# Reading a flag into the engines' registers at the point where it is made, instead of at the end of the kernel

## The chip, the cores and the metric

The kernel runs on one core of one Trainium2 chip. The metric is device time in microseconds (us). It is taken as the median of several executions; before the change three executions took 930.01, 934.81 and 933.51 us, so the median is 933.51 us. One further execution was profiled; its span, from the first instruction to the last, is 929.1 us.

## What is computed

Two blocks follow each other, for 4 sequences (batch 4) of 768 tokens.

The first block is attention with routing, for 8 heads of width 64. Each query and key is assigned to the nearest of 16 centroids, and a query sees only keys of its own cluster. The second block is a feed-forward layer on the joined heads (width 512, hidden width 2048), with a layer norm in front and a residual sum behind:

```python
q_assign = np.argmax(np.einsum('bhsd,hcd->bhsc', q_n, c_n), axis=-1)
k_assign = np.argmax(np.einsum('bhsd,hcd->bhsc', k_n, c_n), axis=-1)
mask = q_assign[:, :, :, None] == k_assign[:, :, None, :]
scores = np.where(mask, scale * q @ k^T, -1e9)
attn = softmax(scores) @ v                     # (B,H,S,D) -> x: (B,S,512)
xn = (x - mu) / np.sqrt(var + 1e-06) * g_ln
out = x + np.maximum(xn @ w_ch1, 0.0) @ w_ch2
```

## The kernel before, in words

**The fast path and its flag.** The kernel computes everything in a fast form that holds only for ordinary inputs: no ties between clusters, and softmax denominators in a safe range. While it runs it collects evidence: `hits` (counts from the routing) and `rdens` (the reciprocals of the denominators). The function `all_in_range()` (lines 735 to 754) folds these into one number, the flag: eleven small VectorE (DVE) instructions make one column `ends` of 128 values, TensorE (PE) turns the column into a row in PSUM (`flag_ps`, L749), and DVE takes its minimum (`flag_f`, L751) and casts it to an integer (`flag`, L753). At the very end the kernel reads the flag (L1008) and, if it is 0, recomputes everything in a slow, general way (`general`, L1009 to 1011). With the inputs of the reference the flag is 1, and the general part does not run.

**Reading the flag.** `nc.values_load` gives every engine that must branch a register with the flag. It is not one instruction but one TENSOR_LOAD on each of the five instruction streams (PE, DVE, ACT, POOL, SP), each of which waits until the cast L753 has run. On SP two bounds instructions follow it. The branches of L1009 and L1010 stand at the end.

**The order of the work.** First comes attention, for 16 pairs of heads, until about 343 us; with it the weights are converted from 64-bit floats. Then comes the feed-forward part, one sequence b after the other (b = 0 to 3). Within a sequence there is a first layer (L774 matmuls, eight units) and a second layer (L867 matmuls). Both use a scheme of fewer block products, at the price of extra sums of blocks on DVE. In the second layer each of six parts (numbered 1, 2, 5, 6, 7, 4, 3 in the order of use, with part 1 ahead of the loop) multiplies three row tiles, 8 matmuls each, so that a part is 24 matmuls of the program. In the trace each of these 32-bit matmuls is two MATMUL records, 48 a part.

**Who sets the order.** Most of the first layer of b = 0 stands in a block of its own whose order is written out for PE, DVE and ACT. All of the rest of the feed-forward part, from the second layer of b = 0 to the end, stands under `tc.manual_schedule(engines={mybir.EngineType.PE})`. That means: PE keeps the order in which the program is written, and the order of DVE, ACT, POOL and SP is chosen by a planner from the dependences. An instruction for PE that is written at some place inside this block therefore stands at that place in PE's stream. The flag load of the kernel before stands behind the block, and so the planner places it on all five streams.

**Around the change.** Between part 1 and part 2 of the second layer of b = 0 the program writes, in this order: the sums `hidden_sums(c, False)` (L861, L862, L863 on DVE), the weight sum `w2_sum(st, 2)` (L851 on DVE), `all_in_range()`, the loads for the norm of the next sequence (`norm_load`, `rows_load`), and then the parts 2, 5, 6, 7, 4, 3. Part 2 is the `y_ps` matmuls of L867, part 5 the first `z_ps` ones, and parts 6, 7 and 4 add to `x_ps`. The next sequence's norm statistics (L537, L538 on DVE, from the tiles `xr` that SP loads with L529) are mixed into this stretch; so is the addition of the residual (L878, L890 on DVE) and the store of the output (L882 on SP).

Of the kernel before, what the change touches and what calls it, by code (L numbers as in the profile page):

```python
# [19 lines left out]
def kernel(  # L20
# [11 lines left out]
    nc = tc.nc  # L32
# [23 lines left out]
    def pool(name, bufs, **kw):  # L56
        return stage.enter_context(tc.tile_pool(name=name, bufs=bufs, **kw))
# [12 lines left out]
    def ps(name, dt=F32, n=512):  # L70
        return pools["t"].tile([P, n], dt, tag="t", name=name)
# [449 lines left out]
    def norm_load(b):  # L521
        xn = norm_tiles(b)[0]
        for c in range(NDC):
            nc.sync.dma_start(out=xn[:, c, :], in_=xT_d[b][c])
# [70 lines left out]
    def w1_sums(b, j, which=range(4)):  # L595
        if 0 in which:
            t = xpool.tile([P, 4, NDH, P], F32, tag="ws", name="ws", bufs=2)
            sets[b, j] = {"s": [t[:, i] for i in range(4)], "all": t}
        t = sets[b, j]["all"]
        for i, (x, op, y) in enumerate((  # L600
            (w1_block(1, 0, j), ALU.add, w1_block(1, 1, j)),
            (t[:, 0], ALU.subtract, w1_block(0, 0, j)),
            (w1_block(0, 0, j), ALU.subtract, w1_block(1, 0, j)),
            (w1_block(0, 1, j), ALU.subtract, t[:, 1]),
        )):
            if i in which:
                nc.vector.tensor_tensor(t[:, i], x, y, op)
# [127 lines left out]
    def all_in_range():  # L735
        ends = small.tile([P, 2], F32, tag="ends", name="ends")
        every = rdens.rearrange("p r e -> p (r e)")

        nc.vector.tensor_reduce(ends[:, 0:1], every, AX.X, ALU.add)
        nc.vector.tensor_reduce(ends[:, 1:2], every, AX.X, ALU.min)  # L740
        nc.vector.tensor_single_scalar(ends[:, 0:1], ends[:, 0:1], WIDE, op=ALU.is_le)
        nc.vector.tensor_single_scalar(ends[:, 1:2], ends[:, 1:2], 1.0 / WIDE, op=ALU.is_ge)
        nc.vector.tensor_tensor(ends[:, 0:1], ends[:, 0:1], ends[:, 1:2], ALU.min)
        for op, op1 in ((ALU.max, ALU.is_le), (ALU.min, ALU.is_ge)):
            nc.vector.tensor_reduce(ends[:, 1:2], hits, AX.X, op)
            nc.vector.tensor_single_scalar(ends[:, 1:2], ends[:, 1:2], float(NG), op=op1)
            nc.vector.tensor_tensor(ends[:, 0:1], ends[:, 0:1], ends[:, 1:2], ALU.min)
        fp = ps("flag_ps")
        nc.tensor.transpose(fp[:1, :P], ends[:, 0:1], ident)  # L749
        flag_f = small.tile([1, 1], F32, tag="flag_f", name="flag_f")  # L750
        nc.vector.tensor_reduce(flag_f, fp[:1, :P], AX.X, ALU.min)  # L751
        flag = const.tile([1, 1], I32, name="flag")
        nc.vector.tensor_copy(flag, flag_f)  # L753
        return flag
# [45 lines left out]
    def relu(m):  # L800
        for h in summed[:m]:
            nc.scalar.activation(h, h, AF.Relu)  # L802
        del summed[:m]
# [35 lines left out]
    def w2_sum(st, i):  # L839
        if i in (1, 3):  # L840
            st["t", i] = xpool.tile([P, NFH, MH], F32, tag="sums", name=f"w2t{i}", bufs=2)
        elif i == 2:
            st["t", 2] = xpool.tile([P, NFH, MH], F32, tag="sums", name="w2t2", bufs=2)
        o, x, y = {
            1: lambda: (st["t", 1], w2_block(0, 1), w2_block(0, 0)),
            2: lambda: (st["t", 2], w2_block(1, 1), st["t", 1]),
            3: lambda: (st["t", 3], w2_block(1, 1), w2_block(0, 1)),
            4: lambda: (st["t", 2], w2_block(1, 0), st["t", 2]),
        }[i]()
        for c in range(0, NFH, 2):  # L850
            nc.vector.tensor_tensor(o[:, c : c + 2], x[:, c : c + 2], y[:, c : c + 2], ALU.subtract)  # L851
# [41 lines left out]
    def second_layer(b, tt, part, st):  # L893
        if part == 1:
            st["x", tt] = ps("x_ps")
            second_product(st["x", tt], tt, (0, 0), w2_block(0, 0), True)
            st["p1", tt] = add_rows(b, 0, tt, 0, st["x", tt])
        elif part == 2:
            y = ps("y_ps")
            second_product(y, tt, (0, 1), w2_block(1, 0), True)  # L900
            add_store(b, 0, tt, 0, st["p1", tt], y)
        elif part == 5:
            st["z", tt] = ps("z_ps")
            second_product(st["z", tt], tt, (1, 0), st["t", 1], True)
        elif part == 6:
            second_product(st["x", tt], tt, (0, 0), st["t", 2], False)
            st["u2", tt] = add_rows(b, 0, tt, 1, st["x", tt])
        elif part == 7:
            second_product(st["x", tt], tt, ("s3",), st["t", 3], False)
            st["u3", tt] = add_rows(b, 1, tt, 1, st["x", tt])  # L910
            add_store(b, 1, tt, 1, st["u3", tt], st["z", tt])
        elif part == 4:
            second_product(st["x", tt], tt, (1, 1), st["t", 2], False)
            store(b, 1, tt, 0, add_rows(b, 1, tt, 0, st["x", tt]))
        elif part == 3:
            second_product(st["z", tt], tt, (0, 1), w2_block(1, 1), False)
            add_store(b, 0, tt, 1, st["u2", tt], st["z", tt])


    def first_units(b, j):  # L920

        chunks = within.pop(j, []) if b == 0 else []
        for part, ahead in ((1, 0), (2, 0), (4, 1), (6, 0), (3, 1), (5, 0), (7, 0)):
            if chunks and part in (1, 3):
                split_weight(chunks[0])
            if j >= ahead:
                first_layer(b, j - ahead, part)
            if part in (4, 6, 3):
                relu(1)
            if chunks and part in (2, 3):  # L930
                m = chunks.pop(0)
                join_weight(m)
                load_weight(m + 2)

            if part == 5 and j + 1 < NFH:
                w1_sums(b, j + 1)
# [18 lines left out]
    with tc.manual_schedule(engines={mybir.EngineType.PE}):  # L955
        for b in range(B):
            st = {}
            if b:
                w1_sums(b, 0)
                for j in range(NFH):  # L960
                    first_units(b, j)
            else:
                rest.close()
                ffn = pool("ffn", 2)
            relu(len(summed))
            w2_sum(st, 1)
            more = b + 1 < B
            for tt in range(TH):
                second_layer(b, tt, 1, st)
                if tt == 0:  # L970
                    first_layer(b, NFH - 1, 4)
                    first_layer(b, NFH - 1, 3)
            relu(len(summed))
            for c in range(NFH):
                hidden_sums(c, False)
            w2_sum(st, 2)
            if b == 0:
                flag = all_in_range()
            if more:
                norm_load(b + 1)  # L980
                rows_load(b + 1, 0)
            for part in (2, 5, 6, 7, 4, 3):
                for tt in range(TH):
                    second_layer(b, tt, part, st)
                    if part == 6 and tt == 0 and more:
                        norm_stat_rows(b + 1)
                if part == 2:
                    for c in range(NFH):
                        hidden_sums(c, True)
                if part == 5:  # L990
                    w2_sum(st, 3)
                if part == 6:
                    w2_sum(st, 4)
                if more and part in (2, 5):
                    for tt in range(TH):
                        norm_rows(b + 1, (0 if part == 2 else TH) + tt)
                    if part == 5:
                        norm_stats(b + 1)
                if more and part == 7:
                    for i in range(2):  # L1000
                        for c in range(NDC):
                            norm_apply(b + 1, i, c)
                if more and part == 4:
                    for i in range(1, 5):
                        x_sum(b + 1, i)

    stage.close()
    usual = nc.values_load(flag[0:1, 0:1], min_val=0, max_val=1)  # L1008
    with tc.If(usual == 0):  # L1009
        with tc.For_i(0, B, 1) as b:  # L1010
            general(tc, b, q, k, v, out, cT, rev, eps, ident, g_sb, w1, w2)
# [194 lines left out]
```

## Time and profile before

| what | value |
|---|---|
| median of three executions | 933.51 us (930.01 to 934.81) |
| span of the profiled execution | 929.1 us |
| DVE busy | 614.6 us (66%) |
| ACT busy | 349.8 us (38%) |
| POOL busy | 78.3 us (8%) |
| PE busy from 400 us to 900 us | all of it, in every stretch asked for |
| last matmul ends | about 924.2 us |
| last DVE instruction (`o_sb`, L890) | 924.18 to 924.61 us |

The page gives the busy time of each engine and its share of the span. Its "chain that ended last" follows the work back from the last instruction: at each step to what released it, or to the instruction before it on the same engine. The view of waits lists, for an engine, whom it stood still for, with the total, the number of times and the longest. A timeline lists instructions in order: start, length, engine, line, operation, output and input tiles, how many are merged in the row, and in square brackets any idle time before it. A "q" behind the engine's name (PEldq, DVEq) means the engine's instruction queue, which handles register loads and the issue of transfers; these are not counted as busy time of the engine. PEld is PE's loading of weights, which runs beside its matmuls.

### The profile page before, as it was taken

Reading aid. Unit: us, or ns where it says so; the run is one execution under the profiler, and the core shown is the slowest. Engines: PE = TensorE matmul, PEld = TensorE weight load, DVE = VectorE, ACT = ScalarE, POOL = GpSimd, SP = SyncE. Lnnn points to the kernel's source line nnn. Section 1 sums busy time; section 2 is a strip of 40 time slices with the busy share of each in tenths; the row PEclk is TensorE's granted clock in tenths of the full one; section 3 lists DMA queues with packets and bytes.
Section 4 is the critical chain, followed back from the end, with each engine's and each line's share of the span. In section 5 each row is a group of like instructions: output and inputs, shape, how many; then the busy total and the mean of one; then the engine's idle time right before and its main releaser. Section 6 shows DMA issues by size and latency. Waiting matters only on the chain.

```text
span 929.1 us, 12604 instructions
## 1 busy us (share of the span) xinstructions
PE 918.7 (99%) x4670; PEld 589.1 (63%) x4670; DVE 614.6 (66%) x1104; ACT 349.8 (38%) x551; POOL 78.3 (8%) x146
## 2 busy tenths in 40 slices
PE   8999999999999999999999999999999999999997
PEld 5444444444444445568886558886557887556886
DVE  4988999999899978889772436472346372434331
ACT  4677777767777653330003331002331001332000
POOL 2121222211211112110000000000000000000000
PEclk9999999999999999999999999999999999999999
DMA  7576888999888455645530002120002021000011
GB/s 153 128 162 125 183 177 166 210 185 166 175 175 162 100 119 142 159 91 170 176 112 8 1 0 94 55 74 17 1 0 86 18 96 40 0 1 6 30 46 37
DMA packets 177061, 89.35 MB, mean 96 GB/s; under 512 B 144096, under 2 KB 160592, under 8 KB 176992
## 3 DMA queue, kind: packets, MB, share of 16 engines
q1 hardware_dynamic: 167648, 73.06, 32.8%
q0 software_dynamic: 7744, 15.02, 8.1%
q8 instruction: 39, 0.64, 0.3%
q10 hardware_dynamic: 1600, 0.39, 0.2%
q14 instruction: 30, 0.25, 0.1%
HBM read 62.52 MB, written 17.52 MB: 86 GB/s over the span
## 4 chain that ended last, share of the span: by engine, by line
PE 92%; DVE 3%; DMA 3%; issue 1%; SPq 1%; ACT 0%; DVEq 0%; ACTq 0%
PE x_ps L867 18%; PE x_ps L774 18%; PE s_ps L407 13%; PE a_ps L419 12%; PE z_ps L867 9%; PE z_ps L774 9%; PE y_ps L867 4%; PE y_ps L774 4%; PE den_ps L456 1%; DMA v_sb<-in_v_dram 1%; PE sim_ps L313 1%; DVE es L436 1%; DMA raw<-in_moe_w_ch_dram 1%; PE simT_ps L329 1%; PE oh_ps L355 1%
## 5 line engine op out<-in xcount | busy, mean ns | idle before, releaser
L402 ACT ACTIVATE e<-s_ps 128x768 f32<-128x768 f32 x192 | 151.6, 811 | 24.3 <-PE s_ps L407 21.8
L407 PE MATMUL s_ps<-t,t 64*128 64x384 f32 x768 | 155.1, 483 | 0.0
L436 DVE TENSOR_TENSOR es<-es,e 128x768 f32<-128x768 f32 x128 | 122.7, 958 | 13.4
L419 PE MATMUL a_ps<-e,v_sb 128*64 128x384 f32 x768 | 130.9, 490 | 0.0
L419 PEld LDWEIGHTS a_ps<-e,v_sb 128*64 128x64 f32 x768 | 52.3, 137 | 70.0 <-issue 59.0
L794 DVE TENSOR_TENSOR h<-z_ps,u 128x384 f32<-128x384 f32 x64 | 35.6, 557 | 91.7 <-PE z_ps L774 69.2
L407 PEld LDWEIGHTS s_ps<-t,t 64*128 64x128 f32 x768 | 68.1, 188 | 35.0 <-issue 34.4
L867 PE MATMUL x_ps<-w2t,h 128*128 128x256 f32 x384 | 84.5, 379 | 0.0
L802 ACT ACTIVATE h<-h 128x384 f32<-128x384 f32 x96 | 49.5, 522 | 85.8 <-DVE h L794 85.8
L867 PEld LDWEIGHTS x_ps<-w2t,h 128*128 128x128 f32 x384 | 72.8, 190 | 10.1
L407 PE MATMUL s_ps<-m,mask 64*128 64x384 bf16 x192 | 62.1, 324 | 1.6 <-ACT e L402 1.2
L407 PE MATMUL s_ps<-mask,m 64*128 64x384 bf16 x192 | 62.0, 324 | 0.4 <-DVE mask L378 0.4
L789 ACT COPY u<-x_ps 128x384 f32<-128x384 f32 x64 | 30.6, 478 | 75.1 <-PE x_ps L774 75.1
L878 DVE TENSOR_TENSOR o_sb<-x_ps,xb 128x256 f32<-128x256 f32 x48 | 20.2, 422 | 49.8 <-PE x_ps L867 49.8
L789 ACT COPY p<-x_ps 128x384 f32<-128x384 f32 x32 | 14.9, 467 | 97.4 <-PE x_ps L774 97.4
L774 PE MATMUL x_ps<-xn,w 128*128 128x384 f32 x128 | 46.6, 487 | 0.6 <-ACT late L445 0.6
L774 PE MATMUL x_ps<-xt,ws 128*128 128x384 f32 x128 | 46.6, 487 | 0.0
L774 PE MATMUL x_ps<-xt,w 128*128 128x384 f32 x128 | 46.5, 486 | 0.0
L774 PE MATMUL x_ps<-xn,ws 128*128 128x384 f32 x128 | 46.5, 486 | 0.0
L774 PE MATMUL z_ps<-xt,ws 128*128 128x384 f32 x128 | 46.5, 486 | 0.0
L774 PE MATMUL z_ps<-xn,ws 128*128 128x384 f32 x128 | 46.5, 486 | 0.0
L774 PE MATMUL y_ps<-xn,w 128*128 128x384 f32 x128 | 46.5, 486 | 0.0
(147 smaller groups left out, 1350.7 us busy)
## 6 DMA issues: line engine op xcount, KB each, us to landing
raw<-in_moe_w_ch_dram SPq DMA_DIRECT2D x32, 512.0 KB, 5.3
w<-tb POOLq DMA_DIRECT2D x32, 256.0 KB, 5.8
v_sb<-in_v_dram SPq DMA_DIRECT2D x32, 192.0 KB, 4.8
xr<-x_d SPq DMA_DIRECT2D x24, 256.0 KB, 2.8
xb<-x_d SPq DMA_DIRECT2D x48, 128.0 KB, 2.2
out_dram<-o_sb SPq DMA_DIRECT2D x48, 128.0 KB, 1.7
k_sb<-in_k_dram SPq DMA_DIRECT2D x62, 96.0 KB, 5.9
rb<-row POOLq DMA_DIRECT2D x30, 192.0 KB, 4.4
```

The lines of the kernel that those rows point to most:

```text
L313: nc.tensor.matmul(sim[r : r + Q, :HC], cT[:, pr, :, :].rearrange("p j c -> p (j c)"), prepared[n][side][:, g * HC : (g + 1) * HC], start= ...
L329: nc.tensor.transpose(simT[:, c * P : (c + 1) * P], sim_sb[:, c * P : (c + 1) * P], ident)
L402: nc.scalar.activation(e, s[:, :, :HC], AF.Exp, scale=SCALE)
L407: nc.tensor.matmul(s[:, j, :HC], of_keys[:, keys], of_queries[:, cols], start=part == first, stop=part != first, skip_group_check=True,)
L419: nc.tensor.matmul(acc[j * D : (j + 1) * D, :HC], loaded[n]["v"][:, j, c, :], e[:, j, :], start=(c == 0), stop=(c == NT - 1),)
L436: nc.vector.tensor_tensor(es, es, soft.pop(i), ALU.add)
L774: nc.tensor.matmul(bank[:, :HC], lhs[:, c, :], rhs[:, c, :], start=first and c == 0, stop=c == NDH - 1, skip_group_check=True,)
L789: nc.scalar.copy(t, bank[:, :HC])
L794: nc.vector.tensor_tensor(h, bank[:, :HC], other, ALU.add)
L802: nc.scalar.activation(h, h, AF.Relu)
L867: nc.tensor.matmul(bank[:, :MH], hidden[lhs + (c,)][:, tt * P : (tt + 1) * P], rhs[:, c, :], start=first and c == 0, stop=c == NFH - 1, sk ...
L878: nc.vector.tensor_tensor(o, bank[:, :MH], x, ALU.add)
```

## The change

The flag load moves from behind the feed-forward block into it, directly behind the call that makes the flag. Its purpose is that the engines have the flag in a register long before the end, so that the branch at the end waits for nothing.

```diff
             w2_sum(st, 2)
             if b == 0:
                 flag = all_in_range()
+                usual = nc.values_load(flag[0:1, 0:1], min_val=0, max_val=1)
             if more:
                 norm_load(b + 1)
                 rows_load(b + 1, 0)
...
     stage.close()
-    usual = nc.values_load(flag[0:1, 0:1], min_val=0, max_val=1)
     with tc.If(usual == 0):
         with tc.For_i(0, B, 1) as b:
             general(tc, b, q, k, v, out, cT, rev, eps, ident, g_sb, w1, w2)
```

Nothing is computed differently, and no arithmetic is added or removed.

## The prediction

> **What bounds the kernel now.** I read the page first, then PE's waits, then the timeline around the flag.
>
> ```profile
> PE 918.7 (99%) x4670; PEld 589.1 (63%) x4670; DVE 614.6 (66%) x1104; ACT 349.8 (38%) x551; POOL 78.3 (8%) x146
> PE 92%; DVE 3%; DMA 3%; issue 1%; SPq 1%; ACT 0%; DVEq 0%; ACTq 0%
> ```
>
> The first line is the busy time by engine, the second the chain that ended last. PE is busy for 99% of the span and makes 92% of the chain. The kernel is a single row of matmuls, so time in which PE stands still is time that nothing can give back.
>
> ```profile
> PE s_ps L407 <- ACT e L402: 1.2, 2, 0.6
> PE idle_ps L649 <- DVE warm L168: 1.0, 1, 1.0
> ```
>
> These head the list of PE's waits over the whole run: total, times, longest. The longest single wait is 1.0 us. The same view from 427 us to the end is empty: after the flag is made, PE waits for nobody until its last matmul. So there is no wait there that a delay could take over.
>
> Now the timeline, in which the change falls (one excerpt for PE, one for DVE):
>
> ```profile
> 427.09 0.27 PE L749 MATMUL flag_ps<-ident,ends 128*1 128x128 f32 x1
> 427.20 7.07 PE L867 MATMUL y_ps<-w,h 128*128 128x256 f32 x32
> ```
>
> ```profile
> 426.80 1.96 DVE L863 TENSOR_TENSOR h<-h,h 128x384 f32<-128x384 f32 x4
> 428.67 0.43 DVE L878 TENSOR_TENSOR o_sb<-x_ps,xb 128x256 f32<-128x256 f32 x1
> ...
> 430.07 0.56 DVE L863 TENSOR_TENSOR h<-h,h 128x384 f32<-128x384 f32 x1
> 430.54 1.90 DVE L851 TENSOR_TENSOR w2t<-w,w2t 128x512 f32<-128x512 f32 x3
> 432.35 0.27 DVE L751 TENSOR_REDUCE flag_f<-flag_ps 1x1 f32<-1x128 f32 x1
> 432.55 0.40 DVE L890 TENSOR_TENSOR o_sb<-y_ps,o_sb 128x256 f32<-128x256 f32 x1
> 432.88 0.13 DVE L753 CAST flag<-flag_f 1x1 int32<-1x1 f32 x1
> 432.94 1.26 DVE L537 BATCH_NORM_STATS2 bn<-xr 128x6 f32<-128x512 f32 x2
> ```
>
> PE makes `flag_ps` at 427.1 us and goes straight on with the `y_ps` matmuls. DVE is five microseconds behind: it has a full row of sums ahead of the reduction L751, and the cast that ends the flag is done at 432.88 + 0.13 = 433.01 us. The flag is therefore not there when PE passes the place where the program writes it.
>
> Last, the flag's own tile: where each stream reads it now.
>
> ```profile
> L1008 POOLq TENSOR_LOAD <-flag x1: 493/493/493, 433.0 to 433.0; - x1
> L1008 SPq TENSOR_LOAD <-flag x1: 497/497/497, 434.6 to 434.6; - x1
> L1008 ACTq TENSOR_LOAD <-flag x1: 461/461/461, 856.2 to 856.2; - x1
> L1008 PEldq TENSOR_LOAD <-flag x1: 484/484/484, 920.1 to 920.1; - x1
> L1008 DVEq TENSOR_LOAD <-flag x1: 541/541/541, 924.2 to 924.2; - x1
> ```
>
> A load takes 461 to 541 ns. PE's runs at 920.1 us, four microseconds before its last matmul ends at 924.2: its queue reaches it while matmuls are still in flight. So it costs nothing today.
>
> **What the Trainium skill says.** "Trainium Architecture — The Big Picture", section "Inside one NeuronCore": each engine runs its own stream of instructions and they meet only through semaphores. The trace agrees: POOL reads the flag at the moment the cast ends, ACT 423 us later. "DMA: Bandwidth & Descriptors", section "Latency and other measured facts", gives about 600 ns as the least for such a register load; this trace shows 461 to 541 ns, and I use these. "TensorE: Matmul & The Clock Gate", section "What's actually happening": TensorE's clock runs at half rate by default, is opened after about one busy window of 3.4 us, and falls back after an idle window of that length; the windows run freely. The trace agrees at the kernel's end, where PE stops at 924.2 us (windows; the columns end with the granted clock, DMA share and GB/s):
>
> ```profile
> 926.00:927.00 1.00, 0.00 (x0) 0.00 (x0) 0.00 (x0) 0.00 (x0) 0.00 (x0) 1.00 0.09 16
> 927.50:928.00 0.50, 0.00 (x0) 0.00 (x0) 0.00 (x0) 0.00 (x0) 0.00 (x0) 0.62 0.00 0
> 928.00:929.00 1.00, 0.00 (x0) 0.00 (x0) 0.00 (x0) 0.00 (x0) 0.00 (x0) 0.50 0.02 8
> ```
>
> A mean of 0.62 over half a microsecond means that 0.38 us of it were at half clock, so the clock fell at 927.6 us, 3.4 us after PE stopped. At the start it agrees too: PE begins at 1.00 us, the `q` transposes from 3.9 to 5.2 us take a median of 421 ns, and the same operation later (L286) takes 273 ns; the `k` transposes from 5.9 us on reach 272 ns. The recovery takes 4.2 to 4.9 us of work.
>
> **The change part by part.**
>
> *Where the loads go.* In the order of the built program, the loads of DVE, ACT and POOL keep their places (behind the last `o_sb`, behind the last relu, and behind the last weight transfer): the planner puts them where it did before. SP's moves two transfers earlier in its stream, still at the cast. PE alone follows the written order, so its load now stands between `flag_ps` and the first `y_ps` matmul and waits for the cast. Behind it in PE's queue are all the matmuls that are left, about 500 us of them.
>
> *The wait.* `flag_ps` ends at 427.36 us. What DVE does up to the reduction is in the same order in both programs, and waits for no `y_ps` result, so the reduction still starts at 432.35. Between it and the cast the planner now puts one L537 instead of the L890 (which would have waited for `y_ps`): 432.55 + 0.60 (two L537 take 1.27 us, overlapping a little) = 433.15 for the start of the cast, 433.28 for its end. The load: + 0.48 = 433.76. Then 0.1 us to the next instruction (SP shows 0.1 between its load and what follows) and 0.21 us from weight load to matmul (426.88 to 427.09 at `flag_ps`): the first `y_ps` matmul at about 434.1 instead of 427.20, so **6.9 us** later. All of it is on the path. Bounds: 6.4, if the cast goes before the L537 and the restart is quick; 7.5, if the restart is slow.
>
> *The clock.* PE stands for 6.7 us, about twice the 3.4 us after which the clock fell at the end of this run. I expect it to fall to half. The matmuls that follow then run at half speed until it rises again; each microsecond of that loses half a microsecond. The start of the trace gives up to 4.9 us, so 2.4 us lost; the skill's windows allow 3.4 us, 1.7 lost. I take the middle, about 4.4 us of half clock, **2.2 us** lost. Bounds: 0 (the windows fall so that the clock stays up, or rises at once) and 3.4 (an estimate: two of the skill's windows of 3.4 us, at half).
>
> *What is gained.* At the end nothing: PE's load was hidden behind its own matmuls, DVE's stays behind the last `o_sb`, and the last store goes out after that `o_sb` as before. In the stretch of the stall DVE can do its L537 and L538 earlier, but no wait of PE existed after 427 us, so this frees no time on the path.
>
> *What moves on SP and DVE.* The planner puts more `xr` loads and norm statistics ahead of the `y_ps` sums. DVE stood 1.7 us at most for such a load in this stretch, and z of part 5 needs PSUM banks only 10.4 us after the `y_ps` restart. Cost 0; 2 us at most.
>
> Sum: 6.9 + 2.2 + 0 = 9.1 us. 933.5 + 9.1 = 942.6 us.
>
> **The rivals.**
>
> *Not slower.* PE's load might run ahead in its queue without holding the matmuls, or the wait might replace idle time. For it: PE's load at 920.1 us did run beside matmuls in flight. Against: there it ran only ahead of older matmuls' ends, nothing was queued behind it, and its wait had been satisfied since 433 us; and PE has no idle time to replace. The time would be 933.5, or 933.0 if the 0.48 us of PE's load count at the end.
>
> *The wait alone, no clock loss.* 933.5 + 6.9 = 940.4. For it: the windows run freely, and a break of 6.7 us just under two of them can straddle one without filling it; and the clock could rise in a partly busy window. Against: 6.7 us hold at least one whole window of 3.4 us nearly always.
>
> *The wait, the clock, and a knock-on.* DVE, with L537 ahead of the `y_ps` sums waiting for `xr` loads in a chain of some 3 us each (2.8 us median from issue to landing), comes late with the sums of part 2 or `w2t`, and PE waits again: up to 2 us, 944.6, or 946 with the clock's upper bound. For it: L537 waited for `xr` five times, 7.4 us in all, between 420 and 490 us. Against: PE itself is then 9 us later, and DVE is busy for only 49 of the 63 us from 427 to 490 (windows).
>
> **How the numbers follow.** Chances: main case 0.70, the wait alone 0.13, the knock-on 0.10, not slower 0.07. The likeliest gives 942.6 us. The range: the wait alone at its lower bound from the median is 939.9, and executions before lie up to 3.5 us under their median and 1.3 above; I take 937.5 as the low end and 946.0 as the high one. Within 0.5% (4.7 us) lie most of the not-slower case and a small part of the wait alone: 0.06; faster by more than that: 0.02; slower: 0.92.
>
> **What would show it.** Right: a wait of PE of 6 to 7 us for DVE's cast at the first `y_ps`, PE's TENSOR_LOAD at 433.3 us, granted clock near 0.5 for some 4 us after it, the following parts shifted by one constant and no other new wait, the same 5 us from the last matmul to the end. Wrong: `y_ps` following `flag_ps` within a microsecond; a clock of 1.00 throughout; or a second wait of PE in parts 5 to 4 of b = 0.

## The result, and the profile after

The changed kernel is slower: 939.88 us in the median of six executions (938.72 to 943.39), against 933.95 us (930.01 to 936.96) for the kernel before, a ratio of 1.0069 with a 95% interval of 1.0041 to 1.0097. The prediction was 942.6 us, with a range of 937.5 to 946.0. The same kernel timed once more, with 29 executions of the kernel before beside it, came to 940.15 against 931.85 us, ratio 1.0098 (1.0073 to 1.0123).

The profiled execution has a span of 936.9 us. First the busy time by engine on its page:

```profile
PE 920.1 (98%) x4670; PEld 589.8 (63%) x4670; DVE 615.4 (66%) x1104; ACT 350.2 (37%) x551; POOL 78.6 (8%) x146
```

PE has as many matmuls as before and 1.4 us more of busy time. The rest of the loss must be idle time, and PE's waits (who waits for whom: total, times, longest) name it at their head:

```profile
PE y_ps L867 <- DVE flag L753: 6.5, 1, 6.5
PE s_ps L407 <- ACT e L402: 1.2, 2, 0.6
```

There is one new wait, 6.5 us for DVE's cast of the flag. The timeline shows it in place (start, length, engine, line, operation, tiles; in brackets the idle time before):

```profile
426.30 0.27 PE L749 MATMUL flag_ps<-ident,ends 128*1 128x128 f32 x1
...
431.52 0.27 DVE L751 TENSOR_REDUCE flag_f<-flag_ps 1x1 f32<-1x128 f32 x1
431.72 0.67 DVE L537 BATCH_NORM_STATS2 bn<-xr 128x6 f32<-128x512 f32 x1
432.32 0.12 DVE L753 CAST flag<-flag_f 1x1 int32<-1x1 f32 x1
...
433.02 12.79 PE L867 MATMUL y_ps<-w,h 128*128 128x256 f32 x48 [6.45 <-DVE flag L753]
```

PE makes `flag_ps`, and then stands until DVE has worked through its queue, reduced the row, taken one norm statistic in between and cast the flag. The flag's own tile shows the loads:

```profile
L979 POOLq TENSOR_LOAD <-flag x1: 487/487/487, 432.5 to 432.5; - x1
L979 PEldq TENSOR_LOAD <-flag x1: 487/487/487, 432.5 to 432.5; - x1
L979 SPq TENSOR_LOAD <-flag x1: 497/497/497, 432.8 to 432.8; - x1
L979 ACTq TENSOR_LOAD <-flag x1: 464/464/464, 864.3 to 864.3; - x1
L979 DVEq TENSOR_LOAD <-flag x1: 543/543/543, 932.3 to 932.3; - x1
```

PE's load has come forward from 920.1 us, and SP's by 1.8 us; those of ACT and DVE are as late as before. Last, the windows around the wait (busy time by engine, then the granted TensorE clock, DMA share, GB/s):

```profile
427.00:429.00 2.00, 0.00 (x0) 0.00 (x0) 2.00 (x5) 0.00 (x0) 0.00 (x0) 1.00 0.02 7
429.00:431.00 2.00, 0.00 (x0) 0.00 (x0) 2.00 (x5) 0.00 (x0) 0.00 (x0) 0.91 0.24 66
432.00:433.00 1.00, 0.00 (x0) 0.01 (x1) 1.00 (x4) 0.00 (x0) 0.00 (x0) 0.50 0.00 0
434.00:435.00 1.00, 1.00 (x4) 0.81 (x3) 0.66 (x2) 0.00 (x0) 0.00 (x0) 0.50 0.76 203
437.00:438.00 1.00, 1.00 (x5) 0.86 (x4) 0.37 (x2) 0.00 (x0) 0.00 (x0) 0.76 0.63 205
438.00:439.00 1.00, 1.00 (x7) 0.87 (x6) 0.56 (x1) 0.00 (x0) 0.00 (x0) 1.00 0.74 137
```

The clock falls at about 430.6 us (0.91 over two microseconds leaves 0.36 us at half), 4.1 us after PE stopped, and is back at about 437.5 us, 4.5 us after it started again. In the fully half-clocked microsecond from 434 us PE starts three matmuls, 0.43 us apart, in the full-clocked one from 438 us five, 0.22 us apart (the counts x4 and x7 take in matmuls that are still running).

The single executions differ in the stretch ahead of the flag: `flag_ps` starts between 426.3 and 429.7 us in the profiled executions of this study that have it behind part 1. Therefore I compare profiles from `flag_ps` on:

| kernel | `flag_ps` starts | first `y_ps` | first `z_ps` less first `y_ps` | `flag_ps` to end |
|---|---|---|---|---|
| before | 427.09 | 427.20 | 10.36 | 502.0 |
| changed | 426.30 | 433.02 | 12.64 | 510.6 |
| changed, once more | 428.07 | 434.73 | 12.71 | 510.6 |
| load behind part 2 | 429.72 | 429.83 | 10.36 | 501.9 |
| load behind one tile | 427.36 | 427.47 | 15.02 | 506.4 |
| changed, PE kept busy | 426.93 | 433.61 | 10.43 | 508.5 |
| PE's wait alone | 427.73 | 433.96 | 12.75 | 510.4 |

Read from the table, the change costs 6.6 us from `flag_ps` to `y_ps` (6.72 less 0.11) and 2.3 us in the `y_ps` part (12.64 less 10.36); behind it the end comes 8.6 us later. The 0.3 us between 8.9 and 8.6 lie behind the last matmul: from the first `z_ps` to the last sum on DVE both kernels take 486.6 us.

### The profile page after: what moved, and what is told of

The parts are those of the page before. It is cut to its first block, busy times and chain, and to the rows that moved or that the text cites. A ratio compares the mean times of both kernels' runs of the same rounds, so it can differ in the third digit from the quotient of the medians.

```text
span 936.9 us, 12600 instructions
## 1 busy us (share of the span) xinstructions
PE 920.1 (98%) x4670; PEld 589.8 (63%) x4670; DVE 615.4 (66%) x1104; ACT 350.2 (37%) x551; POOL 78.6 (8%) x146
## 3 DMA queue, kind: packets, MB, share of 16 engines
q0 software_dynamic: 7744, 15.02, 8.1%
## 4 chain that ended last, share of the span: by engine, by line
PE 96%; DMA 1%; SPq 1%; DVE 1%; ACT 0%; issue 0%; ACTq 0%
PE x_ps L774 18%; PE x_ps L867 17%; PE s_ps L407 16%; PE a_ps L419 14%; PE z_ps L867 9%; PE z_ps L774 9%; PE y_ps L867 5%; PE y_ps L774 4%; PE den_ps L456 1%; PE sim_ps L313 1%; PE simT_ps L329 1%; PE oh_ps L355 1%; SPq L86 1%; DMA xn<-xT_d 1%; DMA v_sb<-in_v_dram 0%; PE qk_ps L286 0%
## 5 line engine op out<-in xcount | busy, mean ns | idle before, releaser
L867 PE MATMUL y_ps<-w,h 128*128 128x256 f32 x192 | 44.4, 393 | 6.5 <-DVE flag L753 6.5
```

The lines of the kernel that those rows point to most:

```text
L867: nc.tensor.matmul(bank[:, :MH], hidden[lhs + (c,)][:, tt * P : (tt + 1) * P], rhs[:, c, :], start=first and c == 0, stop=c == NFH - 1, sk ...
```

## The experiments

My theory: PE's place in the written order makes it wait for the cast, and the wait lets its clock fall. The rivals: the clock has no part in it; the load costs by itself; the other order of DVE and SP costs; the end can gain.

**The change once more.**

> The changed kernel once more, unaltered, timed beside the runs of the others here. Wait and clock: 9 us over the kernel before (6.6 us of wait and restart, 2.4 us of half clock in the y_ps part), or less where the clock falls later or rises sooner; ratio 1.006 to 1.010. Wait alone (no clock loss): 6.6 us over, ratio 1.007.

Measured: 940.15 us, 8.3 us over the kernel before (931.85), the ratio given above.

```profile
428.07 0.27 PE L749 MATMUL flag_ps<-ident,ends 128*1 128x128 f32 x1
434.73 12.87 PE L867 MATMUL y_ps<-w,h 128*128 128x256 f32 x48 [6.39 <-DVE flag L753]
```

The same wait and the same slow `y_ps` part come back. The six executions had a mean granted clock of 0.996 five times and 0.994 once; those of the kernel before 0.998 to 1.000. So the clock's fall is not an accident of one profile.

**The load behind part 2.** Here and in the next experiment the load at the end goes, as in the change.

```diff
                 for tt in range(TH):
                     second_layer(b, tt, part, st)
                     ...
+                if b == 0 and part == 2:
+                    usual = nc.values_load(flag[0:1, 0:1], min_val=0, max_val=1)
```

> The load of all engines is written behind part 2 of the second layer of b = 0, so that PE meets it three y_ps tiles (10.4 us) later, after the cast. Wait theory: no wait of PE and no fall of the clock; within 1 us of the kernel before. Rival, the load on PE costs by itself wherever it stands inside the row of matmuls (drained queue, planner's other order): still 3 to 9 us over the kernel before.

Measured: 930.70 us, ratio to the kernel before 0.9995 (0.9983 to 1.0008).

```profile
429.72 0.27 PE L749 MATMUL flag_ps<-ident,ends 128*1 128x128 f32 x1
429.83 10.53 PE L867 MATMUL y_ps<-w,h 128*128 128x256 f32 x48
440.19 8.15 PE L867 MATMUL z_ps<-w2t,h 128*128 128x256 f32 x37
```

```profile
L988 PEldq TENSOR_LOAD <-flag x1: 492/492/492, 436.3 to 436.3; - x1
```

PE still loads the flag in the middle of its matmuls, at 436.3 us, and `z_ps` follows `y_ps` without a gap: its queue does the load while `y_ps` matmuls are in flight. A load whose flag is there costs nothing that these runs show, so the rival that the load costs by itself falls.

**The load behind one tile of part 2.**

```diff
                     second_layer(b, tt, part, st)
+                    if b == 0 and part == 2 and tt == 0:
+                        usual = nc.values_load(flag[0:1, 0:1], min_val=0, max_val=1)
```

> The load is written behind the first of the three y_ps tiles, so that 3.45 us of matmuls stand between flag_ps and the load. Wait and clock with a whole idle window needed: PE stands 6.5 - 3.45 = 3.0 us, under the 3.4 us, so the clock stays at 1.00; 3.1 us over the kernel before. Rival, the clock falls with any stop of some microseconds: 3.1 + 2 = 5 us over, with a stretch of 0.50 in the granted clock. Rival, the load costs by itself: as the changed kernel.

Measured: 935.49 us, ratio 1.0036 (1.0024 to 1.0047), 3.6 us over the kernel before in the medians.

```profile
427.47 3.62 PE L867 MATMUL y_ps<-w,h 128*128 128x256 f32 x16
433.83 8.83 PE L867 MATMUL y_ps<-w,h 128*128 128x256 f32 x32 [2.74 <-DVE flag L753]
```

```profile
431.10:433.80 2.70, 0.00 (x0) 0.00 (x1) 2.70 (x7) 0.00 (x0) 0.00 (x0) 1.00 0.00 0
433.80:437.40 3.60, 3.57 (x9) 2.85 (x10) 2.39 (x9) 0.00 (x0) 0.00 (x0) 0.53 0.57 179
437.40:442.60 5.20, 5.20 (x26) 4.58 (x25) 3.95 (x10) 0.00 (x0) 0.00 (x0) 1.00 0.27 81
```

The wait shrank by about the tile, as expected. But the clock did not stay up: it fell after a stop of 2.7 us, at about the moment when PE started again, and stayed at half for 3.4 us (a mean of 0.53 over 3.6 us), which costs 1.7. My condition of a whole idle window was wrong. The clock seems not to have fallen each time: of the 16 executions, five have a mean clock of 0.999 (932.78 to 934.20 us), and the eleven with 0.996 to 0.998 took 934.50 to 938.17 us. (A mean of 0.998 alone doesn't prove a fall; five of the 29 executions of the kernel before have it too.) The median lies between my two numbers.

The clock's own record in the traces says more than I read from it. Each complete stretch of one clock is a whole number of times 3.41 us long: 426.67, 6.83 and 498.35 us in the changed kernel, 3.41 us at half here. So the clock changes only at the edges of windows of that length. The window that ended here with the fall (430.53 to 433.94 us) was not idle: PE worked for 0.67 us of it. At the ends of two kernels the clock fell even after a window with 1.30 us of work (load behind part 2, 925.47 to 928.89 us) and stayed up after one with 1.60 us (PE kept busy, 429.02 to 432.43 us). Whether a stop of 2.7 us lets the clock fall should then depend on where it lies among the windows; for the single executions this is argued, since only one of them was profiled.

**PE kept busy through the wait.**

```diff
                 flag = all_in_range()
+                idle = ps("warm_ps")
+                for _ in range(90):
+                    nc.tensor.matmul(idle[:, :P], identb, identb, start=True, stop=True)
                 usual = nc.values_load(flag[0:1, 0:1], min_val=0, max_val=1)
```

> The changed kernel with 90 small matmuls on the identity matrix (their result is not used) between flag_ps and the load, so that PE works through most of the wait. Wait and clock: the y_ps part starts at the same place (6.6 us late, at most 1 us more if the small matmuls run past the cast), but at full clock and takes 10.4 us instead of 12.8; 6.6 us over the kernel before, 2.4 less than the changed kernel. Rival, the slow y_ps part comes from something else than the clock (weights' queue restarting, DMA or DVE traffic beside it): y_ps still takes 12.8 us and the time is that of the changed kernel.

Measured: 938.92 us, ratio 1.0081 (1.0064 to 1.0097), 7.1 us over the kernel before.

```profile
427.04 5.19 PE L981 MATMUL warm_ps<-identb 128*128 128x128 bf16 x90
433.61 10.60 PE L867 MATMUL y_ps<-w,h 128*128 128x256 f32 x48 [1.39 <-DVE flag L753]
```

```profile
433.60:444.10 10.50, 10.49 (x49) 9.26 (x50) 7.79 (x23) 0.30 (x1) 0.00 (x0) 1.00 0.63 174
```

`y_ps` starts 6.68 us after `flag_ps`, as in the changed kernel (6.72 and 6.66), with the same loads and the same traffic beside it (DMA share 0.63 against 0.62). Yet the clock is 1.00 and the part takes 10.43 us instead of 12.64. So the slow `y_ps` part comes from the clock, and not from the late start, the loads or the traffic. In the medians the difference to the changed kernel is only 1.2 us, with six executions of each; the profiles, which leave out the stretch ahead of the flag, show 2.1 us (510.6 less 508.5).

**PE's wait alone.**

```diff
                 flag = all_in_range()
+                nc.values_load(flag[0:1, 0:1], engines={mybir.EngineType.PE})
```

The five loads at the end stay.

> The kernel before with one load more: PE alone also reads the flag at the changed place (its value is not used); the five loads at the end stay. Wait theory: PE's stream is all that counts; PE waits 6.4 us and the y_ps part runs half-clocked, 8.6 us over the kernel before as in the changed kernel (from flag_ps to the end 510.6 us against 502.0). Rival, SP's earlier load or the planner's other order of DVE and SP makes part of the loss: 1 to 3 us less than the changed kernel.

Measured: 939.46 us, ratio 1.0078 (1.0057 to 1.0098), 7.5 us over the kernel before; from `flag_ps` to the end 510.4 us.

```profile
427.73 0.27 PE L749 MATMUL flag_ps<-ident,ends 128*1 128x128 f32 x1
433.96 12.91 PE L867 MATMUL y_ps<-w,h 128*128 128x256 f32 x48 [5.96 <-DVE flag L753]
```

```profile
L979 PEldq EVENT_SEMAPHORE  x1: 51/51/51, 433.9 to 433.9; - x1
```

The trace shows at L979 no TENSOR_LOAD but a wait on the semaphore alone: a load whose value nobody uses was not kept. That makes the test sharper than I meant. PE's wait by itself, 6.0 us, brings back all but 0.2 us of the loss; the load's own half microsecond is the difference between 6.0 and the 6.4 to 6.5 us of the changed kernel. SP reads the flag at 434.8 us here, for the load written at the end, as in the kernel before (434.6), and the loss is there all the same; so the rival of SP's earlier load falls too. DVE has the order of the changed kernel here as well (one L537 between reduction and cast), so this run can't tell DVE's order from the wait. What speaks against a cost of that order beyond the wait is that PE waits for nobody but the cast, and that 6.6 and 2.3 us leave nothing of the loss.

**The flag made earlier.**

```diff
+            if b == 0:
+                flag = all_in_range()
             relu(len(summed))
             w2_sum(st, 1)
             ...
             if b == 0:
-                flag = all_in_range()
                 usual = nc.values_load(flag[0:1, 0:1], min_val=0, max_val=1)
```

> The flag is made earlier: all_in_range() is written ahead of the second layer of b = 0, so that PE turns the column before part 1 and DVE's cast is done before PE comes to the load, which stays where the change put it. Wait theory: no wait of PE, no fall of the clock; within 1 us of the kernel before. Rival, the place of the load itself costs: 0.5 us for the load or up to 9 us.

Measured: 931.01 us, ratio 0.9996 (0.9984 to 1.0009).

```profile
L753 DVE CAST flag<-flag_f x1: 134/134/134, 414.3 to 414.3; 1x1 int32<-1x1 f32 x1
...
L980 PEldq TENSOR_LOAD <-flag x1: 485/485/485, 422.7 to 422.7; - x1
```

The load stands where the change put it, but the cast is eight microseconds ahead of it. PE has no wait from 400 us to the end. The place of the load is harmless; what cost time was that the flag was not ready there. This version has what the change wanted, at no cost, but also at no gain.

**No flag at all.** The edit takes out the call of `all_in_range()`, the loads and the `If` with the slow way.

> The kernel before without flag, loads, branch and general path (it leaves out the guard and the slow way, so it holds for ordinary inputs only): the most that any placing of the loads could gain. My account (the loads at the end are hidden behind matmuls and behind the last sum and store): at most 0.6 us less than the kernel before, of which 0.1 is flag_ps. Rival, the change's idea (the end waits for the flag's loads and branches): 1 us or more less, with a shorter stretch from the last matmul to the end than 4.7 to 4.9 us.

Measured: 929.35 us, ratio 0.9974 (0.9965 to 0.9983), 2.6 us less than the kernel before. This is a miss of mine: I had allowed 0.6. The last DVE instruction shows where most of it is:

```profile
924.49 0.42 DVE L890 TENSOR_TENSOR o_sb<-z_ps,o_sb 128x256 f32<-128x256 f32 x1 [3.03 <-PE z_ps L867]
```

From its start to the end of the span (927.6) are 3.1 us, against 4.9 us in the kernel before (924.18 to 929.1). So the guard does cost 1.8 us at the end of these two profiles; where the other 0.8 us of the medians lie, of which `flag_ps` is 0.1, stays open. The records of the branch, L1009 in the kernel before, show a part of it:

```profile
L1009 SPq EVENT_SEMAPHORE  x8: 17/17/17, 925.5 to 927.4; - x8
L1009 POOLq COMPARE_BRANCH  x1: 45/45/45, 433.6 to 433.6; - x1
L1009 POOLq EVENT_SEMAPHORE  x1: 17/17/17, 433.8 to 433.8; - x1
L1009 ACTq COMPARE_BRANCH  x1: 50/50/50, 856.8 to 856.8; - x1
L1009 ACTq EVENT_SEMAPHORE  x1: 17/17/17, 859.2 to 859.2; - x1
...
L1009 DVEq COMPARE_BRANCH  x1: 76/76/76, 924.8 to 924.8; - x1
...
L1009 DVEq EVENT_SEMAPHORE  x1: 21/21/21, 928.0 to 928.0; - x1
```

DVE branches at 924.8 us and comes to its next instruction only at 928.0. It cannot branch before its last sum. But the branch is not alone at the end. SP waits at L1009 until 927.4 us for the last store to land, and then goes through a second row of waits at the kernel's last line, L1201, until 928.2 us; one of them is for DVE. Here is that row in the kernel before and in the changed one (shortest, median and longest record in ns):

```profile
L1201 SPq EVENT_SEMAPHORE  x14: 17/28/63, 927.5 to 929.0; - x14
L1201 SPq EVENT_SEMAPHORE  x14: 17/28/627, 934.7 to 936.9; - x14
```

In the kernel before SP stands for DVE for at most 63 ns: DVE's branch and SP's own row are over at almost the same time, and either alone would keep the end where it is. On SP's side the 1.8 us are these: without the guard the wait for the last store is over 1.7 us after the store's issue instead of 2.8, and SP's last step follows it by 0.1 us instead of 0.9. Why the store takes longer with the guard is not shown. In the changed kernel the store takes 1.9 us, and SP stands 0.6 us for DVE, whose gap is 3.0 us (932.9 to 935.9). The end is 4.6 us there: the load that was moved is not what the end waits for.

**The price of loads among matmuls.** The kernel before with 54 more loads on PE in b = 1 to 3, one behind each row tile of the six parts that follow part 1 (the second layer has seven parts in all).

> The kernel before with 54 more loads of the flag on PE alone, one behind each of the row tiles of parts 2 to 3 of b = 1 to 3, long after the cast, so that none has to wait (values not used): the price of a load inside the row of matmuls. Hidden (PE's queue reaches a load some microseconds before the matmuls ahead of it are done): 0 to 2 us over the kernel before. Exposed at its full length of 0.48 us each: 26 us over; exposed with restart of the weights as well: 35 us or more.

Measured: 931.65 us, ratio 0.9995 (0.9985 to 1.0004). It does not answer its question: the trace shows 54 semaphore waits of 51 ns at that line and no loads, since their values are not used. It shows only that a wait which is already satisfied costs PE nothing.

**Is it the length of the jump?** "Runtime: NRT & Kernel Launch" of the Trainium skill, section "Instruction fetch mechanics", says that a taken branch to a place outside the instructions fetched ahead has to fetch them first. I made the code that the branch jumps over shorter, once by cutting the slow way to one head, once by rolling it into a loop over pairs of heads.

```diff
-        for h in range(H):
+        for h in range(1):
```

> The kernel before with the slow way shortened to one of its eight heads (it leaves out seven heads of the slow way, which does not run here), so that the code that DVE's branch at the end jumps over is much shorter; flag, loads and branches stay where they are. In the kernel before, DVE's next record comes 3.2 us after its branch (924.8 to 928.0), and without the guard the end was 1.8 us shorter. If that is the jump over a long stretch of code: the gap after DVE's branch falls to well under 2 us and the time by 1 to 2 us. Rival, it is the branch or the load itself, however far it jumps: the gap stays 3 us and the time that of the kernel before.

Measured: 931.92 us, ratio 1.0002 (0.9989 to 1.0014).

```profile
L1009 ACTq COMPARE_BRANCH  x1: 45/45/45, 856.5 to 856.5; - x1
L1009 ACTq EVENT_SEMAPHORE  x1: 17/17/17, 857.0 to 857.0; - x1
...
L1009 DVEq COMPARE_BRANCH  x1: 76/76/76, 924.6 to 924.6; - x1
...
L1009 DVEq EVENT_SEMAPHORE  x1: 21/21/21, 927.7 to 927.7; - x1
```

```diff
-        for h in range(H):
+        with tc.For_i(0, H // 2, 1) as pr:
+          for jh in range(2):
...
```

The lines that index the heads (marked by dots) follow suit.

> The kernel before with the slow way written as a loop over four pairs of heads instead of eight heads one after the other; nothing is left out. Jump-length theory: as with the slow way cut to one head, 1 to 2 us less than the kernel before, or nothing if the shorter code is still too long. Rival: the time of the kernel before.

Measured: 932.29 us, ratio 1.0004 (0.9990 to 1.0018); DVE's gap is 925.1 to 928.2 us, ACT's 857.0 to 857.5.

DVE's gap stays at 3.1 us in both, so a shorter jump, as far as I shortened it, doesn't help DVE. But ACT's gap falls to 0.5 us in both, from 2.4 us in the kernel before (2.4 to 2.7 in the nine profiles with the full slow way). The traces also show transfers of instructions, 8 KB each. In the kernel before one lies in ACT's gap (it starts at 857.7 us); with the slow way shortened the first one comes after the gap (857.6 us). So for ACT the length of the jump makes the difference, as the page says. In DVE's gap such a transfer starts 1.1 us after the branch in all three kernels. DVE's 3 us may therefore be a fetch as well, which these two edits did not avoid; no run shows that. The medians could not have shown a gain anyway: in these two profiles SP waits for the last store until 927.3 and 928.7 us, and the end comes 5.5 and 5.9 us after DVE's last sum.

> The kernel with the slow way rolled into a loop, with the branch turned round so that the slow way runs after the fast one (both are computed, the slow one's output stays). No theory hangs on its time, which is that of the fast way and the slow one together, several milliseconds.

Measured: 3742.25 us, so the slow way adds 2.8 ms. Its trace limits what was said of the clock: here the clock also fell after windows in which PE, with much narrower matmuls (64x16), was busy for up to 3.17 of 3.41 us. The 1.30 and 1.60 us above are thus no general bound.

## Why the prediction was right

**The wait.** Predicted 6.9 us from the old to the new start of `y_ps`, measured 6.6. The chain was the predicted one, down to the L537 between reduction and cast. What was a little too large is the restart: from the end of the load (432.5 + 0.49 = 433.0) to the first `y_ps` matmul I had put 0.3 us, and the trace shows next to nothing.

**The clock.** Predicted 4.4 us at half after the restart and 2.2 us lost; measured 4.5 us and 2.3. That it is the clock is shown by the run with PE kept busy. The idle-window rule that the prediction took from the Trainium skill needs a correction: the stop of 2.7 us behind one tile should have been too short for a whole idle window of 3.4 us, and the clock fell all the same. Its use here holds, because in the changed kernel a whole window (427.23 to 430.65 us) was idle. That the size fits is partly luck. The clock was at half for two windows, 6.83 us, and how much of that falls behind the restart depends on where the stop lies among the windows: 4.5 us here, 4.6 and 4.7 in the other two profiles with a long wait. The 3.4 us from PE's last matmul to the fall at the kernel's end were chance in the same way: it is 2.1 us with the load behind part 2 and 4.8 us with the slow way shortened. The rival "the wait alone" falls with this.

**No knock-on.** Right: from `y_ps` on PE waits for nobody, although DVE waited for `xr` ten times (9.8 us in all, from 427 to 500 us) instead of five (7.4 us). The stretches behind follow at the old distance.

**The end.** Right for the change: the stretch from the last DVE sum to the end is 4.6 us against 4.9. But my reason, that the guard costs next to nothing there, was wrong. The loads are hidden; what follows them, DVE's branch and SP's waits, is not, and without the guard the end is 1.8 us shorter. This change doesn't touch that.

**The sum.** Predicted 9.1 us, found 8.6 in the profiles, 8.3 and 5.9 in the two comparisons of medians. The predicted time of 942.6 us is 2.7 above the measured 939.88. Half a microsecond is the sum (9.1 for 8.6); 1.7 us are the base, for which I took a median of three executions, 933.5, where 29 executions gave 931.85. With both, 931.85 + 8.6 = 940.5; the last 0.6 us are within the spread of the executions. What makes executions of one kernel differ ahead of the flag was not studied.

**What stays open.** Why DVE's branch takes 3 us even with the shorter jump, where 0.8 us of the guard's 2.6 lie, and how much work, and of which kind, a window needs for the clock to stay up.

## What to carry to other kernels

An instruction that reads a value into a register is a wait on the engine's own queue: before it goes to an earlier place, look up when the value is ready and what is queued behind it, above all on the engine that bounds the kernel and whose order is written by hand. Making the value earlier, or reading it one part later, cost nothing here; reading it where it is "made" in the program's text may be microseconds before it is made on the chip. A stop of TensorE can cost more than its length, because the matmuls behind it may run at half clock: here a third more. A guard at the end is not free because its load is hidden: look at what each engine does behind the branch.

## What was not expected of the hardware

The clock fell after a stop of 2.7 us, at the end of a window of 3.41 us in which PE had still worked for 0.67. Every complete stretch of one clock, full or half, is a whole number of such windows. The first record behind a taken branch comes 2.9 to 3.2 us later on DVE, 2.4 to 2.7 on ACT and 0.2 on POOL; with less code to jump over, ACT's came after 0.5 us, and DVE's was not earlier. A register load whose value is not used is not in the trace; its wait is.
